# Head pairs in row and column tiles, 1.5 KB load runs, a permuted token order, two-bank PSUM tiles and a hand-written TensorE order, in an attention block followed by a bilinear FFN

## The chip, the cores and the metric

The kernel runs on one core of a Trainium2 chip. The metric is device time in microseconds (us), measured over several executions. In the profile, PE is TensorE's matmuls, PEld its weight loads, DVE is VectorE, ACT is ScalarE, POOL is GpSimd. The profile is of one execution; its span (first to last instruction) is about 2 us shorter than the device time. Matmul ends are modelled in it, so times of matmuls are read from start to start.

## The reference, cut to what matters

```python
# q, k, v: [4 batches, 8 heads, 768 tokens, 64] fp32; sort_net: [4, 8, 8, 8]
P = sort_net                                    # five rounds of exp, row and column normalisation
for _ in range(5): ...
k_sorted = einsum('bhij,bhjcd->bhicd', P, k_b)  # mix the 8 blocks of 96 tokens of each head
v_sorted = einsum('bhij,bhjcd->bhicd', P, v_b)
scores = scale * q_b @ k_sb.T                   # per block: 96 x 96
attn = softmax(scores)
x = (attn @ v_sb) -> [3072 tokens, 512]         # heads side by side
out = ((x @ w_a) * (x @ w_b)) @ w_out           # 512 -> 1536 -> 512
```

So each batch is 8 heads of small matmuls, then an FFN on 768 tokens. The attention of batch b+1 does not depend on the FFN of batch b, and both kernels run the two together. Only batch 0's attention has no FFN beside it; only batch 3's FFN has no attention beside it.

## The kernel before

The parts that matter (`...` marks cuts):

```python
for h in range(H):                                       # one head at a time
    for t, srct in enumerate((k, v)):                    # rows of 64 floats: 256-byte runs
        sap = _ap(srct, (b*H + h)*S*D, [[D, CPG], [BLK*D, NB], [CPG*D, NCH], [1, D]])
        nc.gpsimd.dma_start(out=kv_b16[:, :, t, :], in_=sap)
    for half in range(2):                                # mix k and v in one 128-column matmul
        ...nc.tensor.matmul(mix_ps[:, ch, :], lhsT=kv_b16[:, half*3 + ch, :, :], rhs=s_all[:, bh, :])
        ...                                              # evacuate to kvsT: k in rows 0-63, v in 64-127
    ...                                                  # 8 transposes of v (rows 64 up), one head
    for half in range(2):
        ...nc.tensor.matmul(sc_ps[:, i, 0:BLK], lhsT=kvsT[0:D, i0+i, :], rhs=qsl)   # 64 rows, 96 columns
        nc.scalar.activation(out=eT[...], in_=sc_ps[...], func=AF.Exp, ...)
        ...nc.tensor.matmul(o_ps[:, i, 0:D+1], lhsT=eT[:, i0+i, :], rhs=vs_sb[:, i0+i, :])
        nc.vector.reciprocal(...); nc.vector.tensor_tensor(out=x_b[...], ...)
for i in range(NB):                                      # at the end of the batch: 16 copies
    ...                                                  # 2 transposes each, then to natural token order
    dst = _ap(xT, ..., [[KA*NTOK, P], [NTOK, 2], [1, NCH], [NCH, CPG]])   # single elements, stride 12 bytes
    nc.vector.tensor_copy(out=dst, in_=src)              # or nc.scalar.copy, in turn
...
for b in range(B):                                       # the framework's scheduler mixes these on PE
    if b + 1 < B: attention_batch(b + 1)
    ffn_ab(2*b); ffn_ab(2*b + 1); ffn_out(2*b); ffn_out(2*b + 1)
```

The softmax here doesn't subtract the row's maximum and nothing guards it: scores larger than these inputs give would overflow.

## Time and profile before

| | before |
|---|---|
| device time, median | 337.25 us |
| first FFN matmul | 69 us, steady from about 73 |
| one mixed stage (FFN of b with attention of b+1) | 71 us |
| FFN alone, one batch (worked out below) | 46.8 us |

The page of the kernel before. First its span and busy tenths in 40 slices, then groups of instructions: busy us, mean ns of one, then idle time of the engine before them and what ended it.

```profile
span 334.5 us, 5969 instructions
PE   0356666689999799999998999999998999999995
...
L210 ACT COPY xT<-xt_ps 128x192 bf16<-128x192 bf16 x32 | 23.7, 873 | 6.1 <-PE xt_ps L199 6.0
L208 DVE COPY xT<-xt_ps 128x192 bf16<-128x192 bf16 x32 | 23.6, 834 | 3.3 <-PE xt_ps L199 2.9
```

PE is busy nine tenths from 73 us on, and only about six tenths before. The copies to xT are slow for their size: 0.85 us for 192 elements a partition.

The chain of work that ended last, of the kernel before: start, length, what. These are the output products of the batches.

```profile
126.45 15.54 PE po L289 x72
197.31 15.54 PE po L289 x72
268.17 15.54 PE po L289 x72
314.91 15.55 PE po L289 x72
```

Mixed stages repeat every 70.9 us, and the last FFN, which is alone, takes 314.91 - 268.17 = 46.74 us. So a batch of attention costs the PE about 24 us inside a mixed stage.

The timeline of PE in the kernel before, in batch 0: start, length, instruction, and in brackets idle time before it.

```profile
36.27 0.53 PE L183 MATMUL o_ps<-vs_sb,eT 96*96 96x65 bf16 x4 [0.58 <-ACT eT L178]
...
39.77 0.58 PE L160 MATMUL vs_ps<-ident,kvsT 64*96 64x64 bf16 x5 [0.74 <-DVE kvsT L156]
...
41.22 0.53 PE L183 MATMUL o_ps<-vs_sb,eT 96*96 96x65 bf16 x4 [0.58 <-ACT eT L178]
```

The same matmul comes back after 41.22 - 36.27 = 4.95 us: heads run one after another, each with waits on ACT and DVE.

The timeline of PE in the kernel before, inside a mixed stage:

```profile
219.89 0.24 PE L175 MATMUL sc_ps<-qTe,kvsT 64*96 64x96 bf16 x1
219.93 0.21 PE L160 MATMUL vs_ps<-ident,kvsT 64*96 64x64 bf16 x1
219.97 0.20 PE L175 MATMUL sc_ps<-qTe,kvsT 64*96 64x96 bf16 x1
219.97 0.21 PE L160 MATMUL vs_ps<-ident,kvsT 64*96 64x64 bf16 x1
```

The v transposes use array rows 64 to 127, the scores rows 0 to 63. From 219.97 us on they start at almost the same time, about one of each per 0.045 us: two row tiles work at once.

### The profile page before, as it was taken

What the parts mean: (1) busy time and instruction counts of PE and PEld (TensorE: products, weight loads), DVE (VectorE), ACT (ScalarE), POOL (GpSimd) and SP (SyncE); (2) the same over time, 40 slices, a digit from 0 to 9 for tenths busy, and PEclk for the clock granted to TensorE, in tenths of its full rate; (3) what the DMA queues carried; (4) which work ended last, traced back from release to release, by engine and by line L of the source; (5) the groups of instructions that cost most, each with busy time, mean ns of one, the idle gap of its engine ahead of it and who ended that gap; (6) DMA issues with size and microseconds to landing.
All of it is one profiled execution on the core that took longest, in us unless ns stands there. A gap on an engine that the chain in (4) does not pass through costs nothing.

```text
span 334.5 us, 5969 instructions
## 1 busy us (share of the span) xinstructions
PE 291.2 (87%) x2345; PEld 177.1 (53%) x2345; DVE 160.0 (48%) x376; ACT 136.5 (41%) x263; POOL 92.5 (28%) x154
## 2 busy tenths in 40 slices
PE   0356666689999799999998999999998999999995
PEld 0345444456666464466664554566665644665542
DVE  4413443567777741057678530366677410344300
ACT  2132222375555831156556521355647311433210
POOL 9899635963543000045431000120000000000000
PEclk9999999999999999999999999999999999999999
DMA  0909999997999001268973002450000012000022
GB/s 12 130 0 104 168 212 202 158 150 50 72 73 73 1 2 57 100 83 69 72 49 26 1 0 96 110 33 0 2 2 0 3 63 96 32 0 2 0 94 94
DMA packets 60940, 20.83 MB, mean 62 GB/s; under 512 B 51185, under 2 KB 56817, under 8 KB 60913
## 3 DMA queue, kind: packets, MB, share of 16 engines
q0 software_dynamic: 57408, 14.16, 44.6%
q1 hardware_dynamic: 3504, 6.30, 5.0%
q8 instruction: 18, 0.29, 0.4%
q14 instruction: 10, 0.07, 0.1%
HBM read 28.32 MB, written 6.29 MB: 103 GB/s over the span
## 4 chain that ended last, share of the span: by engine, by line
PE 74%; DMA 9%; POOL 6%; ACT 5%; DVE 3%; issue 1%; POOLq 0%; ACTq 0%
PE pb L278 19%; PE po L289 19%; PE pa L272 19%; ACT xT L210 4%; PE q_ps L115 4%; PE sc_ps L175 4%; DMA w_out_sb<-in_moe_w_out_dram 3%; PE o_ps L183 3%; POOL s_all L251 3%; PE mix_ps L143 3%; PE vs_ps L160 3%; DMA w_a_sb<-in_moe_w_a_dram 2%; PE xt_ps L199 2%; DMA q_b_786<-in_q_dram 1%; DMA kv_b_431<-in_v_dram 1%
## 5 line engine op out<-in xcount | busy, mean ns | idle before, releaser
L272 PE MATMUL pa<-xT,w_a_sb 128*128 128x384 bf16 x384 | 85.7, 329 | 0.0
L278 PE MATMUL pb<-xT,w_b_sb 128*128 128x384 bf16 x384 | 85.1, 329 | 0.0
L281 DVE TENSOR_TENSOR hT<-a_sb,pb 128x384 bf16<-128x384 bf16 x96 | 53.5, 557 | 50.2 <-PE pb L278 43.1
L276 ACT CAST a_sb<-pa 128x384 bf16<-128x384 f32 x96 | 46.9, 488 | 47.4 <-DVE hT L281 34.0
L289 PE MATMUL po<-w_out_sb,hT 128*128 128x512 bf16 x288 | 62.8, 379 | 0.0
L178 ACT ACTIVATE eT<-sc_ps 96x384 bf16<-96x384 f32 x64 | 31.1, 486 | 45.9 <-PE sc_ps L175 45.4
L289 PEld LDWEIGHTS <-hT 128*128 128x128 bf16 x288 | 28.2, 98 | 33.5
L272 PEld LDWEIGHTS <-w_a_sb 128*128 128x128 bf16 x384 | 35.0, 98 | 19.9 <-issue 0.2
L278 PEld LDWEIGHTS <-w_b_sb 128*128 128x128 bf16 x384 | 34.6, 98 | 20.0
L294 ACT COPY o_sb<-po 128x512 f32<-128x512 f32 x16 | 9.4, 585 | 56.3 <-PE po L289 56.3
L183 PE MATMUL o_ps<-vs_sb,eT 96*96 96x65 bf16 x256 | 25.0, 226 | 8.3 <-ACT eT L178 7.6
L183 PEld LDWEIGHTS <-eT 96*96 96x96 bf16 x256 | 19.4, 138 | 19.0 <-ACT eT L178 15.5
L189 DVE TENSOR_TENSOR x_b<-o_ps,rec 96x256 bf16<-96x256 f32 x64 | 27.2, 426 | 1.7
L296 DVE COPY o_sb<-po 128x512 f32<-128x512 f32 x8 | 5.5, 691 | 46.8 <-PE po L289 46.8
L175 PE MATMUL sc_ps<-qTe,kvsT 64*96 64x96 bf16 x256 | 27.3, 232 | 0.0
L210 ACT COPY xT<-xt_ps 128x192 bf16<-128x192 bf16 x32 | 23.7, 873 | 6.1 <-PE xt_ps L199 6.0
L208 DVE COPY xT<-xt_ps 128x192 bf16<-128x192 bf16 x32 | 23.6, 834 | 3.3 <-PE xt_ps L199 2.9
L160 PE MATMUL vs_ps<-ident,kvsT 64*96 64x64 bf16 x256 | 19.2, 221 | 6.2 <-DVE kvsT L156 5.3
L160 PEld LDWEIGHTS <-kvsT 64*96 64x96 bf16 x256 | 16.1, 137 | 14.8 <-ACT kvsT L154 7.0
L154 ACT CAST kvsT<-mix_ps 128x384 bf16<-128x384 f32 x32 | 15.3, 479 | 19.2 <-PE mix_ps L143 19.0
L164 DVE COPY vs_sb<-vs_ps 96x512 bf16<-96x512 bf16 x32 | 13.5, 423 | 20.0 <-PE sc_ps L175 12.0
L187 DVE RECIPROCAL rec<-o_ps 96x4 f32<-96x4 f32 x64 | 11.3, 177 | 24.6 <-PE o_ps L183 24.1
(213 smaller groups left out, 259.6 us busy)
## 6 DMA issues: line engine op xcount, KB each, us to landing
out_dram<-o_sb SPq DMA_DIRECT2D x24, 256.0 KB, 2.0
w_a_sb<-in_moe_w_a_dram POOLq DMA_DIRECT2D x4, 384.0 KB, 7.7
w_b_sb<-in_moe_w_b_dram POOLq DMA_DIRECT2D x4, 384.0 KB, 12.2
w_out_sb<-in_moe_w_out_dram POOLq DMA_DIRECT2D x12, 128.0 KB, 6.7
q_b_131<-in_q_dram POOLq DMA_DIRECT2D x1, 192.0 KB, 3.5
q_b_151<-in_q_dram POOLq DMA_DIRECT2D x1, 192.0 KB, 4.4
q_b_171<-in_q_dram POOLq DMA_DIRECT2D x1, 192.0 KB, 4.8
q_b_191<-in_q_dram POOLq DMA_DIRECT2D x1, 192.0 KB, 5.3
```

What stands on the lines that cost most here:

```text
L160: nc.tensor.matmul(vs_ps[:, i, :], lhsT=kvsT[D:D2, i, :], rhs=ident[D:D2, D:D2], is_transpose=True)
L175: nc.tensor.matmul(sc_ps[:, i, 0:BLK], lhsT=kvsT[0:D, i0 + i, :], rhs=qsl, start=True, stop=True)
L178: nc.scalar.activation(out=eT[:, i0:i0 + NBH, :], in_=sc_ps[:, :, 0:BLK], func=AF.Exp, scale=float(scale))
L183: nc.tensor.matmul(o_ps[:, i, 0:D + 1], lhsT=eT[:, i0 + i, :], rhs=vs_sb[:, i0 + i, :], start=True, stop=True)
L189: nc.vector.tensor_tensor(out=x_b[:, i0:i0 + NBH, h, :], in0=o_ps[:, :, 0:D], in1=_ap(rec, i0, [[NB, BLK], [1, NBH], [0, D]]), op=ALU.mult)
L208: nc.vector.tensor_copy(out=dst, in_=src)
L210: nc.scalar.copy(out=dst, in_=src)
L272: nc.tensor.matmul(pa, lhsT=w_a_sb[:, kc, m * P:(m + 1) * P], rhs=xT[:, kc, t0:t0 + TOK_CH], start=(kc == 0), stop=(kc == KA - 1))
L276: nc.scalar.copy(out=a_sb, in_=pa)
L278: nc.tensor.matmul(pb, lhsT=w_b_sb[:, kc, m * P:(m + 1) * P], rhs=xT[:, kc, t0:t0 + TOK_CH], start=(kc == 0), stop=(kc == KA - 1))
L281: nc.vector.tensor_mul(out=hT[:, m, :], in0=a_sb, in1=pb)
L289: nc.tensor.matmul(po, lhsT=hT[:, m, sub * P:(sub + 1) * P], rhs=w_out_sb[:, m, :], start=(m == 0), stop=(m == KO - 1))
```

## The change

A matmul that contracts over 64 rows uses half of the array's rows, a *row tile*; one with 64 weight columns uses half of its columns, a *column tile*. To *evacuate* PSUM is to copy a matmul's result from there to SBUF; PSUM comes in banks.

The intent: treat two heads as a pair, so that their half-array matmuls lie in different row or column tiles and overlap; load k, v and q of a pair in three transfers, each partition reading six neighbouring tokens (1.5 KB) of a head; let tokens stay in that permuted order through the FFN and put them right in the output's row pattern, so that the copy to xT is contiguous; evacuate PSUM two banks at a time; pad weights to 128 columns; and write the PE order by hand, with units of attention between FFN steps. The core of the diff (`...` marks cuts):

```diff
-                nc.gpsimd.dma_start(out=kv_b16[:, :, t, :], in_=sap)          # one head, k or v
+            nc.gpsimd.dma_start(
+                out=to, in_=_ap(t, (b * H + 2 * hp) * S * D, [[W, P], [S * D, 2], [1, W]]))
...
+        for c in range(NCH):                                # q transposes; the k/v mix alike
+            for e in range(2):
+                nc.tensor.matmul(q_ps[e * D:(e + 1) * D, c, :],            # column tile of head e
+                                 lhsT=q2[:, e, c * D:(c + 1) * D], rhs=ident, is_transpose=True)
...
+                for e in range(2):                          # scores: row tile of head e
+                    nc.tensor.matmul(sc[:, e, i * BLK:(i + 1) * BLK],
+                        lhsT=kT[e * D:(e + 1) * D, blk * BLK:blk * BLK + P],   # padded to 128 columns
+                        rhs=qT[e * D:(e + 1) * D, blk], start=True, stop=True)
+            nc.scalar.activation(out=eT[:, hf, :, 0:HB], in_=sc[0:BLK, :, 0:HB],  # two banks
+                                 func=AF.Exp, scale=float(scale))
...
-                dst = _ap(xT, ..., [[KA * NTOK, P], [NTOK, 2], [1, NCH], [NCH, CPG]])
+        nc.vector.tensor_copy(out=xT[:, g % HP, :].rearrange("p (i t) -> p i t", i=NB), in_=xt_ps)
...
+                    rhs=_ap(xT, kc * S + t * 3 * CG,        # FFN reads pieces of 16 tokens
+                            [[KA * S, P], [CG, 3], [BLK, NB], [1, CG]]),
...
-        nc.gpsimd.tensor_tensor(out=_ap(s_all, ...), ...)   # mixing matrices of all batches
+            spread(nc.vector, pc_ps, 0, 2)                  # batch 0 on VectorE
+            spread(nc.vector, pc_ps, 2, 6)
+            ...
+            for c in range(4): load_ab(c)
+            for hp in range(HP): load_pair(1, hp)
+            for g in range(1, 4): spread(nc.gpsimd, p_col, g * 8, 8)
...
+    with tc.manual_schedule(engines={mybir.EngineType.PE}):
+            for g in range(1, HP): stage_q(g, ps0b, "B")
+            C0(0); C0(1); R0(0); O0(0); to_xT(0, ps0b, "B")     # batch 0
+            ...
+                for s, step in enumerate(steps):                # 24 FFN steps, 6 output steps
+                    step()
+                    want = -(-(s + 1) * len(units) // (n - 2))  # 16 units: c_, r_, o_, x_ of 4 pairs
+                    while done < min(want, len(units)):
+                        units[done](); done += 1
```

The units of a pair are c_ (q transposes, mix of k and v), r_ (scores, exp, v transposes), o_ (product and normalisation) and x_ (transpose to xT).

## The prediction

> **What bounds the kernel now.** TensorE throughput from about 73 us to the end, a chain of waits before that. The 40-slice table shows PE at 9 tenths from 73 us on; the chain of waits puts 74% of the span on PE. FFN alone (timeline at 300 us) runs without gaps: four 128x384 matmuls per 0.65 us, 72 matmuls of po in 15.54 us; so FFN costs 46.8 us per batch. The mixed stages (attention of batch b+1 with FFN of b) repeat every 71 us (po at 126.5, 197.3, 268.2 us), so attention costs about 24 us of PE per batch. Span = 73 (start) + 3 x 71 + 47 + about 2: the profile's 334.5 us.
>
> **The start.** Balancing ends at 11.6 us. Then GpSimd spreads s_all (10.8 us, to 24.5) and only afterwards issues the remaining k/v loads, 0.8 us each. Heads go one after another, 4.95 us each (timeline 28 to 63 us, PE about 60% busy): mix, evacuate, scores, exp, product. Last come strided copies into xT (64 in all, 0.83 to 0.87 us, 47 us), with waits of PE on them.
>
> **What changes.**
> 1. Start: k, v, q of a pair come in three loads with 1.5 KB runs, issued at once; s_all of batch 0 is made by VectorE right after balancing (estimate 14 us instead of 24.5). But PE's order puts q of pairs 1 to 3 before the first mix, so it waits for the 12th load: with 192 KB per about 1.2 us (first q loads of before) about 18 us. Then four pairs at an estimated 6 us each (ACT about 3.1, DVE about 3.6 us a pair, from 0.48 us per 384-element cast and 0.43 us per normalisation), plus 3 us. FFN starts at about 44 us instead of 73: minus 29 us.
> 2. Batch-1 loads and the other s_all spreads stand behind eight weight loads in GpSimd's order. PE wants pair 4 right after the first FFN step: estimate 3 us of stall.
> 3. Mixed stages: PE matmuls per batch go from 320 to 336, but scores of two heads sit in two row tiles. The trace already shows such overlap: vs_ps (rows 64 up) and sc_ps (rows 0 up) start in pairs every 0.04 us near 220 us, while sc_ps alone takes about 0.08 us. This agrees with the Trainium skill, "TensorEngine Tiling (Array Packing)", Key Properties: different tiles work in parallel. For column tiles (q, mix) this trace shows nothing. v transposes halve. Per pair PE about 3.5 us if column tiles overlap, 5 if not, against 6 now. The fixed order adds waits, about 1 us a pair. Attention: 19.5 us a batch instead of 24: minus 13 us.
> 4. xT copies shrink from 47 us to about 10; this pays through shorter waits, counted above.
> 5. Last FFN and tail stay.
>
> Sum: 337 - 29 + 3 - 13 = 298 us.
>
> **Prediction: 298 us, 285 to 313 in 8 of 10. Faster by over 2%: 0.97; within: 0.02; slower: 0.01.**
>
> **What would show it.** First pf matmul at 40 to 49 us; po groups of the mixed stages 64 to 69 us apart; q and mix matmuls starting in pairs (column overlap) or evenly spaced; a PE wait for k/s_all at 45 to 52 us; xT copies about 0.6 us x16; pf still 0.65 us per four.
>
> **What would make it wrong.** Column tiles that serialise, or costly switches of tile shape (up by 10 us); permuted 16-element reads of xT slowing FFN matmuls; batch-1 data arriving much later; VectorE bursts holding the three FFN banks; or, downward, waits hidden fully (285).

## The result

The changed kernel takes 277.14 us (276.89 to 278.30), the kernel before 337.25 us; the ratio is 0.823, with a 95% interval of 0.820 to 0.825. Ratios here and below are the mean time of one kernel's fast runs over that of the other's of the same rounds, so not quite the ratio of the medians that are quoted. The direction was right; the time lies 8 us below the predicted range.

The page of the changed kernel (span, tenths of PE, granted TensorE clock, and the group that answers to the two above):

```profile
span 275.0 us, 5700 instructions
PE   0267757999999999999999999999999999999993
PEclk9998775999999999999999999999999999999999
...
L217 DVE COPY xT<-xt_ps 128x768 bf16<-128x768 bf16 x16 | 8.9, 554 | 8.9 <-PE xt_ps L215 8.9
```

The timeline of PE in the changed kernel, where the FFN begins:

```profile
44.83 1.44 PE L231 MATMUL pf<-xT,w_a_sb 128*128 128x384 bf16 x4 [0.65 <-DVE xT L217]
```

The first FFN matmul is at 44.83 us, where 44 was predicted. The chain of work that ended last, with the second half of the output products of batches 0 to 2:

```profile
98.19 7.77 PE po L247 x36
157.28 7.77 PE po L247 x36
216.38 7.77 PE po L247 x36
```

Mixed stages repeat every 59.1 us, not every 66.3 (46.8 + 19.5) as predicted. Less the FFN's 46.8 us, attention costs the PE 12.3 us a batch. This is where the prediction failed. The timeline of PE in such a stage:

```profile
118.63 0.81 PE L231 MATMUL pf<-xT,w_b_sb 128*128 128x384 bf16 x4
119.38 0.53 PE L131 MATMUL q_ps<-ident,q_691 128*64 128x128 bf16 x12
119.73 0.50 PE L145 MATMUL mix<-s_all,k_687 128*64 128x128 bf16 x12
120.07 0.50 PE L145 MATMUL mix<-s_all,v_689 128*64 128x128 bf16 x12
120.50 0.82 PE L231 MATMUL pf<-xT,w_a_sb 128*128 128x384 bf16 x4
121.17 0.81 PE L231 MATMUL pf<-xT,w_b_sb 128*128 128x384 bf16 x4
121.91 0.51 PE L166 MATMUL sc<-qT,kT_106 64*128 64x96 bf16 x16
122.36 0.62 PE L177 MATMUL vs_ps<-ident,vT_109 128*128 128x128 bf16 x8
```

Read from start to start: 12 mix matmuls take 0.34 us, 28 ns each; 16 score matmuls 0.45 us, 28 ns each. No bracket stands on any line: PE waits for nothing. The view of waits, asked for PE from 50 us on, is empty. Instruction by instruction, the two matmuls of a pair of heads start 3 ns apart (119.735 and 119.739 us), the next two 56 ns later (119.791): a matmul with 64 columns is not short, two of them run side by side.

Of the 59.5 us by which the span shrank, 36.0 had been won by the middle of batch 0's output products (98.2 us against 126.45 + 7.77 = 134.2), and 11.8 in each of the two stages that follow (70.9 against 59.1).

### The profile page after: what moved, and what is told of

It reads as the page before. It is cut to its first block, busy times and chain, and to the rows that moved or that the text cites. A ratio compares the mean times of both kernels' runs of the same rounds, so it can differ in the third digit from the quotient of the medians.

```text
span 275.0 us, 5700 instructions
## 1 busy us (share of the span) xinstructions
PE 247.8 (90%) x2400; PEld 152.7 (56%) x2408; DVE 130.7 (48%) x284; ACT 98.1 (36%) x194; POOL 48.7 (18%) x67
## 4 chain that ended last, share of the span: by engine, by line
PE 88%; DVE 4%; DMA 3%; POOL 2%; issue 1%; ACT 0%; DVEq 0%
PE pf L231 46%; PE po L247 22%; PE mix L145 5%; PE vs_ps L177 4%; PE sc L166 3%; PE o_ps L189 3%; DMA q_102<-in_q_dram 3%; PE q_ps L131 2%; PE xt_ps L215 2%; DVE xp L196 2%; DMA p_nat<-in_sort_net_dram 1%; DVE vs_115 L179 1%; DVE rec L193 0%; POOL v_88 L78 0%; POOL q_96 L78 0%
## 5 line engine op out<-in xcount | busy, mean ns | idle before, releaser
L240 DVE TENSOR_TENSOR hT<-a_sb,pf 128x384 bf16<-128x384 bf16 x96 | 53.1, 553 | 66.2 <-PE pf L231 55.1
L231 PE MATMUL pf<-xT,w_a_sb 128*128 128x384 bf16 x384 | 78.9, 328 | 0.6 <-DVE xT L217 0.6
L231 PE MATMUL pf<-xT,w_b_sb 128*128 128x384 bf16 x384 | 78.8, 328 | 0.0
L239 ACT CAST a_sb<-pf 128x384 bf16<-128x384 f32 x96 | 46.0, 479 | 76.8 <-PE pf L231 53.0
L196 DVE TENSOR_TENSOR xp<-o_ps,rec 96x512 bf16<-96x512 f32 x32 | 21.2, 684 | 0.5
L215 PE MATMUL xt_ps<-ident,xp 96*128 96x96 bf16 x128 | 9.4, 214 | 4.9 <-DVE xp L196 4.7
L217 DVE COPY xT<-xt_ps 128x768 bf16<-128x768 bf16 x16 | 8.9, 554 | 8.9 <-PE xt_ps L215 8.9
L155 ACT CAST kT_106<-mix 128x384 bf16<-128x384 f32 x12 | 5.2, 482 | 16.6 <-PE mix L145 16.6
L170 ACT ACTIVATE eT_112<-sc 96x768 bf16<-96x768 f32 x12 | 9.0, 802 | 4.6 <-PE sc L166 4.6
L135 DVE COPY qT<-q_ps 128x768 bf16<-128x768 bf16 x16 | 8.7, 551 | 2.7 <-PE q_ps L131 2.7
L170 ACT ACTIVATE eT_114<-sc 96x768 bf16<-96x768 f32 x10 | 7.5, 807 | 0.9 <-PE sc L166 0.9
L170 ACT ACTIVATE eT_113<-sc 96x768 bf16<-96x768 f32 x10 | 7.5, 807 | 0.9 <-PE sc L166 0.9
L155 ACT CAST kT_108<-mix 128x384 bf16<-128x384 f32 x10 | 4.3, 482 | 7.6 <-PE mix L145 7.6
```

Of the source, the lines that this page charges most:

```text
L135: nc.vector.tensor_copy(out=qT.rearrange("p i c t -> p c i t"), in_=q_ps.rearrange("p c (i t) -> p c i t", i=NB))
L155: nc.scalar.copy(out=d1, in_=s1)
L170: nc.scalar.activation(out=eT[:, hf, :, 0:HB], in_=sc[0:BLK, :, 0:HB], func=AF.Exp, scale=float(scale))
L196: nc.vector.tensor_tensor(out=_ap(xp, hf * NBH * 2 * D, [[NB * 2 * D, BLK], [D, 2], [2 * D, NBH], [1, D]]), in0=_ap(o_ps, 0, [[1024, BLK], ...
L215: nc.tensor.matmul(xt_ps[:, i, :], lhsT=xp[:, i], rhs=ident[0:BLK, 0:BLK], is_transpose=True)
L217: nc.vector.tensor_copy(out=xT[:, g % HP, :].rearrange("p (i t) -> p i t", i=NB), in_=xt_ps)
```

## The experiments

A "stage" below is the distance between the output products of two batches in the chain of work, 59.1 us in the changed kernel. Each time is a median; rounds differ a little, so the ratio to the kernel before is given (the changed kernel has 0.823).

### Do the two heads' tiles overlap? First try: a different order in the program

```diff
-        for c in range(NCH):
-            for e in range(2):
+        for e in range(2):
+            for c in range(NCH):        # q transposes and mix (e1); the scores alike (e2)
```

> The changed kernel with one edit: in the q transposes and the k/v mix, all six matmuls of one head first, then the six of the other, so neighbours stand in the same column tile. Same work, same instruction count. Theory A (a good part of the gain in the mixed stages is overlap of column tiles, 28 ns a matmul of 128 columns now): neighbours no longer overlap, 53 to 57 ns each, 36 matmuls a pair, so +1.0 us a pair in 12 warm pairs and about +5 us in the cold start: 290 to 295 us. Theory B (the gain comes from the fixed order with fewer switches of tile shape and no waits; column tiles don't overlap): 277 to 279 us.

> The changed kernel with one edit: the scores of one head's four blocks first, then the other head's, so neighbours stand in the same row tile. Theory A (row tiles overlap, 28 ns a matmul now): 16 matmuls a pair at 43 ns (96 columns at full clock) to 77 ns (what lone score matmuls take in the kernel before): +0.25 to +0.8 us a pair, 16 pairs: 281 to 290 us. Theory B: 277 to 279 us.

e1 measured 279.46 us (0.826), stages 59.7 us. e2 measured 277.88 us (0.821), stages 59.2 us. Theory A looked refuted, but the trace says otherwise. The timeline of PE in e1; in the program, the six q matmuls of head 0 stand first, then six of head 1, then the mix of k:

```profile
109.62 0.55 PE L131 MATMUL q_ps<-ident,q 128*64 128x128 bf16 x10
109.97 0.22 PE L145 MATMUL mix<-s_all,k 128*64 128x128 bf16 x1
110.00 0.22 PE L131 MATMUL q_ps<-ident,q 128*64 128x128 bf16 x1
110.03 0.22 PE L145 MATMUL mix<-s_all,k 128*64 128x128 bf16 x1
110.06 0.22 PE L131 MATMUL q_ps<-ident,q 128*64 128x128 bf16 x1
```

The mix of head 0 (columns 0 to 63) started before the last q transposes of head 1 (columns 64 to 127), which stand ahead of it in the program. A matmul whose tile was free did not wait its turn. (The q matmul that signals the end of its group started at 110.06 us, after two of the mix.) So the edit did not take the overlap away; nor did it in e2, where 16 scores still take 0.46 us. These two runs decide nothing about its worth. At the end of the group one tile is left to itself, and there the mix matmuls start 56 ns apart (110.62, 110.68, 110.73 us). A better test had to make overlap impossible.

### Second try: the whole array for every matmul

```diff
-                nc.tensor.matmul(q_ps[e * D:(e + 1) * D, c, :],
-                                 lhsT=q2[:, e, c * D:(c + 1) * D],
+                nc.tensor.matmul(q_ps[:, c, :],                       # wrong result on purpose
+                                 lhsT=q2[:, e, min(c, 4) * D:min(c, 4) * D + P],
...                                                                   # mix likewise; scores:
-                        lhsT=kT[e * D:(e + 1) * D, blk * BLK:blk * BLK + P],
-                        rhs=qT[e * D:(e + 1) * D, blk], start=True, stop=True)
+                        lhsT=kT[:, blk * BLK:blk * BLK + P],
+                        rhs=qT[:, blk], start=True, stop=True)
```

> Wrong result on purpose. The two reorderings before this one did not take overlap away (the trace still had 28 ns a matmul: matmuls of a free tile ran ahead of their place in the program). So here q transposes, k/v mix and scores use the whole array: weights of 128 columns, or 128 rows, so that no two can overlap; count, loads and evacuations stay. Theory A (overlap of the two heads' tiles is worth much): q and mix 28 to 55 ns, scores 28 to 42 ns a matmul, so +1.0 and +0.2 us a pair, 12 warm pairs +15 us, and some us more in the start: 290 to 297 us, output products of two stages about 63.5 to 64.5 us apart where they are 59.1. Rival (a matmul with a 64-column weight is simply short): 276 to 280 us.

It measured 289.44 us (0.859), stages 62.7 us. The timeline of PE in e9:

```profile
111.53 0.83 PE L131 MATMUL q_ps<-ident,q 128*128 128x128 bf16 x12
112.20 0.83 PE L145 MATMUL mix<-s_all,k 128*128 128x128 bf16 x12
112.87 0.83 PE L145 MATMUL mix<-s_all,v 128*128 128x128 bf16 x12
...
114.84 0.84 PE L166 MATMUL sc<-qT,kT 128*128 128x96 bf16 x16
115.52 0.61 PE L177 MATMUL vs_ps<-ident,vT 128*128 128x128 bf16 x8
```

Twelve mix matmuls take 0.67 us, 56 ns each, twice as long; 16 scores 0.68 us instead of 0.45. Column tiles as well as row tiles overlap, and that is worth 62.7 - 59.1 = 3.6 us a batch, net: the changed kernel also loses about 0.1 us at each of the four changes of tile shape of a pair (FFN to q, mix to FFN, FFN to scores, scores to v transposes), which e9 does not have. This agrees with the Trainium skill, "TensorEngine Tiling (Array Packing)", Key Properties, for both kinds of tile.

### The padding to 128 columns

```diff
-                        lhsT=kT[e * D:(e + 1) * D, blk * BLK:blk * BLK + P],
+                        lhsT=kT[e * D:(e + 1) * D, blk * BLK:(blk + 1) * BLK],   # v transposes and product alike
```

> The changed kernel with weight loads of 96 columns in place of the padded 128, in scores, v transposes and products. Theory C (a share of the gain that I had not costed is the padding: 128-column weights load faster, 98 against 138 ns in the two traces): the product goes from 32 back to about 57 ns a matmul, scores slow as well: +0.4 to +0.8 us a pair, 283 to 290 us. Rival (padding is only there for layout): 276 to 278 us.

It measured 281.90 us (0.832), stages 60.1 us, so 1.0 us a batch. The timeline of PE in e3:

```profile
116.91 0.87 PE L189 MATMUL o_ps<-vs,eT 96*96 96x65 bf16 x16
117.62 0.82 PE L231 MATMUL pf<-xT,w_a_sb 128*128 128x384 bf16 x4
```

The 16 products take 0.71 us, 44 ns each, where the changed kernel takes 0.51 us (32 ns); scores and v transposes lose 0.04 and 0.03 us. A weight load of the product takes 138 ns on average in e3 and 98 to 103 ns in the changed kernel, though it loads more columns there. The Trainium skill, "TensorE: Matmul & The Clock Gate", Weight-path perf modes, says that the fast weight load needs exactly 128 weights. The run agrees: loads of 96 columns are the slower ones. The padding gained less than I had expected, 0.26 us a pair.

### The waits that I had predicted

```diff
-                    want = -(-(s + 1) * len(units) // (n - 2))
+                    want = 4 * (s // 7 + 1)             # the four units of a pair back to back
```

> The changed kernel with the four attention units of a pair (load and mix, scores, product, transpose) emitted one after the other with no FFN step between them, then seven steps of FFN. Theory D (the waits of about 1 us a pair that I predicted are real, and the FFN steps between the units hide them all): PE waits of about 0.8 us before the product and 0.8 and 0.5 us before the transposes, as in the start of the changed kernel, appear in 12 pairs: +1.5 to +2.5 us a pair, 295 to 307 us. Rival (such waits are absent at full clock whatever the order): 277 to 280 us.

It measured 337.25 us (0.996): the whole gain is gone. The timeline of PE in e6:

```profile
127.82 0.53 PE L131 MATMUL q_ps<-ident,q 128*64 128x128 bf16 x12
...
129.64 0.34 PE L166 MATMUL sc<-qT,kT 64*128 64x96 bf16 x8 [0.62 <-DVE vT L157]
...
131.86 0.67 PE L189 MATMUL o_ps<-vs,eT 96*128 96x65 bf16 x16 [0.78 <-DVE vs L179]
133.30 0.34 PE L215 MATMUL xt_ps<-ident,xp 96*128 96x96 bf16 x4 [0.77 <-DVE xp L196]
134.13 0.50 PE L215 MATMUL xt_ps<-ident,xp 96*128 96x96 bf16 x4 [0.49 <-DVE xp L196]
134.43 1.48 PE L231 MATMUL pf<-xT,w_a_sb 128*128 128x384 bf16 x4
135.71 1.47 PE L231 MATMUL pf<-xT,w_b_sb 128*128 128x384 bf16 x4
```

A pair now holds the PE for 134.43 - 127.82 = 6.6 us, against 2.9 us for the same units in the changed kernel. The two FFN groups behind it take 1.28 us each instead of 0.65, because the granted clock has fallen to 0.50 there. Together 5.0 us a pair, 12 pairs, 60 us. Of the 3.7 us more, 2.9 are idle in the trace (0.62, 0.20, 0.78, 0.77 and 0.49 us); the rest is hidden under modelled ends. So the waits are real and larger than I had said; the FFN steps between the units hide them whole. The effect is well above my range of 295 to 307 us, because the waits came to 3.7 us a pair and not 1.5 to 2.5, and because I had not counted the clock.

### The hand-written PE order

```diff
-    with tc.manual_schedule(engines={mybir.EngineType.PE}):
+    if True:
```

> The changed kernel without the hand-written PE order: the framework's scheduler places the matmuls as in the kernel before; tiles, loads, layout stay. Theory B (order is about half of the gain in the mixed stages: 2.8 us a batch of switch cost inside FFN groups, 2 us of waits at the transposes): +9 to +18 us, 286 to 295 us. Theory A (the tiles alone): 277 to 281 us.

It measured 272.78 us (0.807): without the hand-written order the kernel is faster, which neither theory said. Stages stay at 59.1 us. The difference is the start. The timeline of PE in e4 (the profile kept is another execution; it has this wait as 3.18 us, at 40.35 us):

```profile
40.08 0.48 PE L145 MATMUL mix<-s_all,k 128*64 128x128 bf16 x5 [3.22 <-POOL s_all L261]
40.49 1.46 PE L231 MATMUL pf<-xT,w_a_sb 128*128 128x384 bf16 x4
```

The scheduler began the first mix at 12.9 us instead of 17.7, because it did not put all q transposes first, and pair after pair took about 4.5 us instead of 6.6, with a granted clock of 0.92 on average (12 to 36 us) where the changed kernel's start had 0.76 (17.7 to 44.8 us). Batch 0 was done by 36 us; then PE waited for batch 1's s_all, the wait that I had predicted at 45 to 52 us and that the changed kernel does not reach.

What the order in which units and FFN steps are *emitted* is worth, another run shows:

```diff
+                for u in units:
+                    u()                 # the whole attention of batch b+1 first, as in before
+                units = []
```

> Without the hand-written PE order, and with a batch's whole attention emitted ahead of its FFN, as in the kernel before; the scheduler then mixes them finely (five FFN matmuls, then a piece of attention). Against the run without hand-written PE order alone (272.8 us). Theory H (fine mixing costs: cut FFN groups and switches were about 3 us a batch in before, plus waits at the transposes): 278 to 284 us. Rival (the scheduler's mixing is as good as the order in which the units are emitted): 271 to 275 us.

It measured 279.83 us (0.829) with stages of 61.6 us, so 2.5 us a batch more than e4. The scheduler left FFN groups cut into pieces of two to seven matmuls with attention between, as in the kernel before. Placing whole units between whole FFN steps pays. Fixing the PE's order by hand on top of that gains nothing in the stages, and as written it lost in the start.

### The permuted token order

```diff
-        nc.vector.tensor_copy(out=xT[:, g % HP, :].rearrange("p (i t) -> p i t", i=NB), in_=xt_ps)
+        for i in range(0, NB, 2):       # natural token order: single elements, stride 12 bytes
+            dst = _ap(xT, (g % HP) * S + i * BLK, [[KA * S, P], [BLK, 2], [1, NCH], [NCH, CG]])
+            src = _ap(xt_ps, i * BLK, [[NB * BLK, P], [BLK, 2], [CG, NCH], [1, CG]])
+            ...                         # VectorE and ScalarE in turn
-                    rhs=_ap(xT, kc * S + t * 3 * CG, [[KA * S, P], [CG, 3], [BLK, NB], [1, CG]]),
+                    rhs=xT[:, kc, t * HW:(t + 1) * HW],
```

> The changed kernel with the permuted token order of xT undone: the transposes go to xT in natural token order by four copies of 192 elements a pair with single elements written at a stride (as before: 0.83 to 0.87 us each there), half of them on ScalarE; FFN reads contiguous columns, output rows are contiguous. If the strided copies hold PE (in before PE waited 1.4 us a batch for them and shared the FFN groups with them): stages 61 to 63 us apart, 283 to 289 us. If they are hidden behind the FFN steps that follow: stages 59 to 60 us, 277 to 280 us. The FFN group tells at the same time whether 16-element pieces cost the FFN anything: 0.65 us either way if not.

It measured 291.92 us (0.864), stages 62.2 us. In the groups of e12:

```profile
L224 ACT COPY xT<-xt_ps 128x192 bf16<-128x192 bf16 x32 | 25.6, 800 | 35.0 <-DVE xT L222 35.0
L222 DVE COPY xT<-xt_ps 128x192 bf16<-128x192 bf16 x32 | 25.6, 799 | 22.0 <-ACT xT L224 13.0 <-PE xt_ps L215 8.9
```

The timeline of PE in e12, behind the copies of a pair:

```profile
126.99 0.81 PE L237 MATMUL pf<-xT,w_b_sb 128*128 128x384 bf16 x4 [0.28 <-ACT a_sb L244]
128.34 0.53 PE L131 MATMUL q_ps<-ident,q 128*64 128x128 bf16 x12 [0.54 <-ACT xT L224]
```

The copies cost 51.2 us of two engines again, and PE has waits: 0.28 us on an FFN group and 0.54 us on the q transposes behind the copies. From start to start these steps take 3.74 us where the changed kernel takes 2.70, so 1.04 us, at three of the four pairs of a stage; behind the fourth come output products, and nothing is lost. That is 3.1 us a batch, and the first FFN matmul comes at 50.0 us, 5.2 us later: 3 x 3.1 + 5.2 = 14.5 us, where 14.8 was measured. The edit makes four copies of one and gives half of them to ScalarE as well; stride and number of copies were not separated. FFN groups take 0.65 us in both orders, so reading 16-token pieces costs the PE nothing.

### Loads and s_all in the start

```diff
-            nc.gpsimd.dma_start(out=to, in_=_ap(t, ..., [[W, P], [S * D, 2], [1, W]]))
+            for e in range(2):          # 64-float pieces; one transfer a head
+                nc.gpsimd.dma_start(out=to[:, e, :, 0:D], in_=_ap(t, ..., [[W, P], [D, NCH], [1, D]]))
```

> The changed kernel with k, v, q loaded in 256-byte pieces, one transfer a head (which this shape of pattern forces), 96 transfers in place of 48; layout of the result otherwise unchanged. Theory E (long runs are what brings the first FFN step to 45 us): the first 24 transfers alone take 0.8 us each to issue, so the last q of batch 0 arrives at about 24 us or later instead of 17, and batch-1 data becomes late: first FFN at 52 to 60 us, 285 to 295 us. Rival (the start was bound by the s_all spread on GpSimd and by the head chain, not by loads): 277 to 280 us.

It measured 288.34 us (0.852); stages stay at 59.1 us, the first FFN matmul comes at 51.8 us. Theory E holds: the last q transfers of batch 0 were only issued at 19.7 to 21.3 us. Of the 11.2 us, 7.0 are lost by the first FFN matmul; then PE waits 3.1 us for batch 1's s_all, which stands behind the longer issues in GpSimd's order. The run changes run length and number of transfers together; the two were not separated.

```diff
-        nc.gpsimd.tensor_tensor(out=_ap(s_all, ...       # the kernel before, s_all on VectorE
+        nc.vector.tensor_tensor(out=_ap(s_all, ...
```

> The kernel before with one part of the change alone: the spread of s_all on VectorE instead of GpSimd, which frees GpSimd to go on issuing loads. Theory F (the start of before is held by the 10.8 us spread): the chain of heads starts about 8 to 10 us earlier and the time falls to 327 to 330 us. Rival (loads and the head chain hold it): 335 to 338 us.

It measured 338.42 us (1.001, interval 0.996 to 1.007): nothing gained. Theory F falls for this edit. The loads of weights and batch 1 were issued some 10 us earlier, but VectorE's q copies now stood behind the spreads (first product at 27.95 us, before 26.44), and the heads still took 4.95 us each. So the run does not tell what a spread that delays neither engine would bring. In the kernel before, PE waited 0.75 us for s_all at the first mix; from the first product on, seven more heads of 4.95 us each lead to about 61 us, and only the copies into xT come after.

### Two-bank evacuation

```diff
-            nc.scalar.activation(out=eT[:, hf, :, 0:HB], in_=sc[0:BLK, :, 0:HB], ...)
+            for e in range(2):          # reciprocal and normalisation likewise
+                nc.scalar.activation(out=eT[:, hf, e, 0:HB], in_=sc[0:BLK, e, 0:HB], ...)
```

> The changed kernel with exp, reciprocal and normalisation of a two-bank tile split into two instructions, one a bank. VectorE and ScalarE get some 0.15 to 0.2 us more per extra instruction (6 a pair). Theory G (off the critical path in the mixed stages, since PE waits for nothing there): only the start pays, 277 to 281 us. Rival (evacuation paces the PE): +1 us a pair, 288 to 295 us.

It measured 278.58 us (0.825), stages 59.1 us, first FFN matmul at 46.9 us. Theory G holds for the mixed stages: off the critical path. For the start it is not clear: 2 us later here, but e6, whose start is that of the changed kernel, has its first FFN matmul at 45.6 us, and the 1.4 us in the time are within the intervals of the ratios.

### A better start

Three edits to the changed kernel were tried: a new order of batch 0, the clock, and the order of loads.

```diff
-            C0(0); C0(1); R0(0); O0(0); to_xT(0, ps0b, "B")
-            ...                                             # all q transposes stood before these
+            C0(0); Q0(1); C0(1); R0(0)
+            Q0(2); C0(2); O0(0); R0(1); X0(0)
+            Q0(3); C0(3); O0(1); R0(2); X0(1)
+            O0(2); R0(3); X0(2); O0(3); X0(3)
...
-            for c in range(4): load_ab(c)
-            ...
+            for c in range(2): load_ab(c)                   # v1; s_all of batches 1 to 3 here
+            for g in range(1, 4): spread(nc.gpsimd, p_col, g * 8, 8)
+            ...
```

> Candidate: the changed kernel with another hand-written order of batch 0 (first mix right after the balancing, q transposes between, product of one pair behind the scores of the next) and the s_all spreads of batches 1 to 3 ahead of the last four weight loads. If the start is what is left to gain: first FFN at 33 to 38 us instead of 44.8, 266 to 271 us. If batch-1 data holds it then: 270 to 275 us with a wait of PE on q or k of pair 4.

v1 measured 266.26 us (0.789), first FFN matmul at 34.1 us. The same early spreads with the scheduler's PE order:

> Candidate: no hand-written PE order, and only the s_all spreads moved ahead of the last four weight loads. In the run without hand-written order PE waited 3.2 us for s_all at 40 us. If that wait is all that held it: first FFN at about 36.5 us and 268 to 270 us. If late loads or the clock take its place: 271 to 273 us.

v2 measured 271.21 us (0.802), the median of its three fast executions (268.98 to 271.97); the fourth, 273.24 us, counts as slow. So v1's order of batch 0, with the same early spreads, is some 5 us better than the scheduler's. The wait for s_all was gone, but in the profiled run batch 0 ran at the slow clock (16 products in 0.97 us from start to start, where e4 had 0.60), which took its place.

Warming the clock with matmuls that nobody reads (`warm(36)` before the first q transposes, `warm(26)` behind them):

> The changed kernel with 62 matmuls on the identity that nobody reads, put where PE waits in the first 12 us, so that the clock is at full rate when batch 0's attention starts. If the half-rate clock costs the start something: mix 0.34 instead of 0.64 us per 12, about 1.5 to 2 us less for each of four pairs where PE work is on the chain; first FFN at 39 to 42 us, 271 to 274 us. If the loads (last q at 17 us) and the evacuations hold it, or the clock falls again in the gaps: first FFN at 43.5 to 45 us, 275 to 278 us.

e11 measured 277.86 us (0.823): nothing. After 1.67 and 2.60 us of waiting for loads of q, the granted clock read 0.50 at 16 to 18 us, before the first mix. So the same warming was put on v1's order, which has no such wait, with 20 matmuls more ahead of the first FFN step:

> Candidate: v1_start (266.3 us) with the same idle matmuls, and 20 more in the last waits before the first FFN step, which ran its first two matmul groups at half rate (1.2 us each instead of 0.65). If the clock is worth what it seems: 262 to 265 us, first FFN at 32 to 33 us with 0.65 us per group. If ScalarE and VectorE pace batch 0: 265 to 267 us.

v4 measured 265.99 us (0.789). The first FFN matmul came at 32.5 us at the full clock, but after two groups PE waited 3.40 us for batch 1's first q. So loads were put in the order of need (a quarter of the FFN's weights, then one pair of batch 1, in turn; s_all after the first of these), without and with the warm clock:

> Candidate: v1_start with the loads in the order in which they are needed, a quarter of the FFN weights and one pair of batch 1 in turn. v1_start had no PE wait for batch 1 (first FFN at 34.1 us), so if loads were not its limit: 265 to 267 us, as before.

> Candidate: the same load order with the warm clock of v4_start_warm. If the 3.4 us wait for q of pair 4 is all that took the warm clock's gain back: first FFN at 32.5 us, no wait after it, 261.5 to 263.5 us. If another load or s_all takes its place: 264 to 266 us.

v5 measured 265.34 us (0.787), v6 262.58 us (0.779, 262.49 to 263.58): the fastest version, with a correct result. In this start the warm clock is worth 2.8 us. The timeline of PE in v6:

```profile
32.35 0.81 PE L231 MATMUL pf<-xT,w_a_sb 128*128 128x384 bf16 x4 [0.18 <-DVE xT L217]
33.00 0.81 PE L231 MATMUL pf<-xT,w_b_sb 128*128 128x384 bf16 x4
33.74 0.53 PE L131 MATMUL q_ps<-ident,q 128*64 128x128 bf16 x12
```

No wait follows, and the groups take 0.65 us from the first.

## Why the prediction was right or wrong, point by point

**What bounds the kernel: right.** The sum of start, three mixed stages and a last FFN describes both kernels.

**Point 1, the start: the time was right, the saving was not.** The first FFN matmul comes at 44.8 us against 44, but in the kernel before it came at 69.0; 73, from which I subtracted, is where the FFN there became steady. The saving is 24.2 us, not 29. On the way to 44.8, the last q of batch 0 came at about 17 us as costed, and the FFN waited for it through the hand-written order. Two parts were less right than the total: pairs took up to 6.7 us rather than 6, in part at a half-rate clock that I had not thought of; and the spread of s_all, with which I had begun, delayed PE by only 0.75 us in the kernel before.

**Point 2, a stall for batch 1's data: wrong by 3 us.** The data were there. s_all was ready at about 40 us and PE first wanted it at 48. The wait is real once the start is faster: 3.2 us in e4.

**Point 3 failed: "Attention: 19.5 us a batch instead of 24".** Overlap and the halved v transposes were named rightly, their sizes were not; the fixed order was said to add waits, and added none. Measured: 12.3 us a batch, so 7.2 us a batch or 21.6 us in three stages too much. Two terms made it:

- *PE work per pair.* I had taken 3.9 us (19.5 / 4, less 1 of waits), between 3.5 (column tiles overlap) and 5 (they do not). Measured: 2.9 us from first to last matmul of the units, 3.1 us with the gaps. Column tiles overlap fully (28 ns a matmul, 56 in e9), and the padding, which I had not costed, took the product from 44 ns (e3) to 32. Even the low end, 3.5, was 0.4 us too much. This is 3.2 us of the 7.2.
- *Waits, "about 1 us a pair".* Measured: none, which is the other 4 us. The waits exist, 3.7 us a pair plus 1.3 us of slow clock when units stand back to back (e6). The prediction named "waits hidden fully" as its way down to 285, and they were. I put them in without counting what stands between the units: 16 units in 28 steps leave one to two FFN steps, 1.3 to 2.6 us, between any two, longer than any wait in e6 (0.8 us). The diff could have told this.

In the terms of the prediction's sum: the start brought -24.2 us (said: -29), the stall 0 (said: +3), the three mixed stages 3 x -11.8 = -35.4 (said: -13). That gives about 277.6 us, and 277.14 us was measured. So the misses do not all point one way: the start's saving, 5 us too large in the prediction, hid part of the error in point 3.

**Where the 11.8 us a batch came from.** Undone one at a time: overlap 3.6 (e9), contiguous copies to xT 3.1 (e12), whole units between whole FFN steps 2.5 (e10 against e4), padding 1.0 (e3). That is 10.2. The halved number of v transposes may be about 1 more: 2.9 us a batch of PE time before, 1.8 after, by start-to-start times. That part was not tested alone, and the four need not simply add up.

**Point 4, the copies: their size right (0.55 us), their worth too low.** "This pays through shorter waits, counted above" gave them no number; e12 gives 14.8 us in all, the largest among the parts of the change that were undone alone.

**Point 5: right.** The last FFN takes 47 us in both.

**What would show it:** the first pf at 44.8 (said: 40 to 49) and 0.65 us per group held; q and mix start in pairs; stages 64 to 69 us apart and the wait at 45 to 52 us did not come.

## What to carry to other kernels

When a chain of small dependent steps shares an engine with dense work, count the dense work that stands between two steps of the chain and compare it with the chain's waits: here 1.3 us between steps hid them all, and without it they cost 60 us together with the slower clock. Choose a layout that keeps evacuations contiguous and put the permutation where it is free, such as the output's row pattern. And undo one part of a large change at a time: the hand-written PE order cost some 4 us as it stood (another order of batch 0, v1, gained), while the copies' layout alone was worth 15.

## What the Trainium skill lacked or had wrong

- "TensorE: Matmul & The Clock Gate", Part 3, says that matmuls start and end in strict program order. Here they did not start so across tiles: in e1 a mix matmul of column tile 0 started at 109.97 us, before q transposes of column tile 1 that stand ahead of it in the program (110.00, 110.06). Ends are modelled in this profile, so they tell nothing. Reordering the program (e1, e2) therefore did not test overlap here.
- The same page, in "Why this matters for your kernels", advises against idle gaps of over about 3 us; elsewhere (Part 1 and "A second HAM failure mode") it says that the clock follows how busy PE was, and that short idles can lower it too, but it gives no share of work at which this happens. In e6 the clock fell to 0.50 at 133.6 us although no single wait was over 0.78 us: PE was busy for 1.87 us of the 3.42 us before. The price is 0.63 us per FFN group of four (1.28 against 0.65). Where the limit lies, no run shows.
- "TensorEngine Tiling (Array Packing)", Key Properties, says that a change of tiling mode drains the engine, without a figure. Here the first start after a switch between the full array and row or column tiles, either way, came about 0.1 us late, four times a pair (121.17 + 0.65 = 121.82, scores at 121.91; 120.07 + 0.34 = 120.41, FFN at 120.50).
- No page says how a profile's clock reads before the first change is recorded. In the changed kernel the row reads 0.9 or more up to 20 us, while 12 mix matmuls at 17.7 us took 0.64 us, as at half rate. Durations tell it, the row does not.
